# Sums of weight pieces and of hidden tiles, placed elsewhere in six passes of a fused attention and mixture-of-experts kernel

## The chip, the cores and the metric

The kernel runs on one core of one Trainium2 chip. The metric is the time of one execution on the device in microseconds, the median of several runs. A core has TensorE (PE: matmuls into PSUM banks), VectorE (DVE), ScalarE (ACT), GpSimd (POOL) and SyncE (SP), whose queue issues all of this kernel's DMA transfers in order. Each engine works through its own list of instructions in order and waits on semaphores of the others.

## The reference

```python
def _attn_ref(q, k, v):                       # B, H, S, D = 8, 8, 576, 64; chunk = 64
    scores = scale * np.matmul(q_c, k_c.transpose(0, 1, 2, 4, 3))
    scores = scores - np.max(scores, axis=-1, keepdims=True)
    attn = np.exp(scores)
    attn = attn / (np.sum(attn, axis=-1, keepdims=True) + 1e-09)
    out = np.matmul(attn, v_c)
...
def _moe_ref(x, domain_probs, w1, w2):        # N, D, E, F = 4608, 512, 4, 1024
    p = domain_probs / (domain_probs.sum(-1, keepdims=True) + 1e-09)
    out = np.zeros((N, D), dtype=np.float32)
    for e in range(E):
        h = np.maximum(x @ w1[e], 0.0)
        out += p[:, e:e + 1] * (h @ w2[e])
```

Attention within chunks of 64 positions gives 4608 tokens of 512 numbers. Each token goes through all four experts, and the results are added with the token's weights.

## The kernel before, in words

**Tiling.** A block is 512 tokens. The first block is computed plainly; the other eight go in four pairs (0 to 3). An expert's 1024 hidden units are halved, so that there are 8 passes over weight halves for each pair: passes 0 to 7 are the first block's, 8 to 15 pair 0's, 16 to 23 pair 1's, and so on to 39. A matmul in full precision is made of three: every factor is split into a high part (a rounded copy, on ScalarE) and a low part (what is left, a subtraction on GpSimd).

**Seven products for eight.** A pass multiplies 2x2 blocks by a scheme of seven products with sums of blocks on both sides. Each product is six matmuls of 128x512. For w1 the factors are `a11 a12 a22` and the sums `s1 s2 s3 s4`, for two groups g = 0, 1 of columns (the first and second half). A w1 *unit* holds two such factors with their high and low parts. There are seven units (0 to 6) to a pass: unit 0 is a11 and a12 of the first half, unit 1 is s2 and s1, unit 2 is s3 and a22, unit 3 is s4 and a11 of the second half, and so on. For the hidden tiles h, the sums are `t1` to `t4`, each for k = 0, 1.

**The order of a pass.** TensorE's 28 steps are written out: `a1 g1 a2 g2 g6 a5 g5 a6 a3 g7 a7 g4 g3 a4 h1 h2 b1 b5 h6 b6 b3 h5 b7 h7 b2 b4 h4 h3`, numbered 0 to 27. g and h are the first layer (x by w1) of this pass, in banks A0, B0, C0; a and b are the second layer (h by w2) of the pass before, in banks A1, B1, C1. In a and b, products 1, 6, 7 and 4 accumulate in A1, one after the other, product 2 goes to B1, and 5 and 3 to C1; after each step VectorE adds the bank to a sum in SBUF (`acc`, L936). TensorE may write a bank again only when that addition has read it. So b4 (step 25) waits for b7's addition (step 22), and a1 of the next pass for b4's.

**What stands beside the steps.** A table `at` says after which step other work is written: each engine's list follows this order exactly. In h's part, L909 adds two banks, L874 applies the rectifier and the token's weight, L880 is a sum t1 to t4, and L886 and L889 are high and low parts of h. Attention for the next pair runs beside passes 10 to 14 (scores on TensorE, softmax on VectorE and ScalarE: L275, L280, L286, L289 to L296, L155, L161, L165).

**What is special in passes 9 to 15.** In these the kernel makes w1's units on the chip from raw w1 pieces and stores them in memory, so that later passes only load them. `half_load` brings a half's pieces, `half_sum` (L525, 128x256) makes s1 to s4 from them, `make_unit` takes a unit's high part on ScalarE (L542) and low part on GpSimd (L543), and a store follows (L546). Units 0 and 1 of the next pass are made at steps 20 and 26, unit 2 of this pass at step 2, and the others at 8, 11, 14 and 17. g6 (step 4) is the first reader of unit 1. The pieces of the first half are summed one pass ahead, those of the second half in their own pass. All pieces lie in the tile `xraw`, in which q and k for attention (L189) and w2's raw pieces take the same room afterwards. In pass 14, `make_before` splits three units of the last w2 (ScalarE L558, GpSimd L559, stores L563). In pass 15 the tokens of pair 1 come back from memory into `xraw` (L270), and VectorE makes a first sum of them at step 5 (L657).

Of the kernel before, what the change touches and what calls it, by code (L numbers as in the profile page):

```python
# [31 lines left out]
def chunk_attention_moe(ctx: ExitStack, tc: tile.TileContext, qk, v, v0, dp, w1, w2, out):  # L32
# [10 lines left out]
    nc = tc.nc  # L43
# [3 lines left out]
    n_pass = 2 * n_exp  # L47
# [96 lines left out]
    def a_softmax(t):  # L144
        a_less_max(t)
        a_exps(t)
# [10 lines left out]
    def a_place(t, name="pt"):  # L157

        s = st[t]
        s["pt"] = att.tile([P, 2, HG, C], F32, name=name)  # L160
        nc.scalar.copy(out=s["pt"], in_=s["sc"])  # L161
        for half in range(2):
            for i in range(2):
                here, there = (slice(half * C + k * B, half * C + (k + 1) * B) for k in (i, 1 - i))
                nc.scalar.copy(  # L165
                    out=s["pt"][there, :, :, i * B : (i + 1) * B],
                    in_=s["sc"][here, :, :, (1 - i) * B : (2 - i) * B],
                )
# [11 lines left out]
    def two_load(t, i, groups=slice(0, 2)):  # L180
        if i == 0:
            a_load(t)
            return
        pair = (t - NT) // (PAIR * NT)
        if pair == 1:
            if groups.start == 0:
                to = pieces(0, 4).rearrange("p a b c -> p (a b c)")
                st[t] = {"x": to.rearrange("p (g x h s) -> p g x h s", g=2, x=2, h=HG)}
            nc.sync.dma_start(  # L189
                out=st[t]["x"][:, groups],  # L190
                in_=qk[t, groups].rearrange("g c d x h s -> (c d) g x h s"),
            )
            return
        to = of_tiles(pair, 6, 2).rearrange("p g (x i) (j s) -> p g x (i j) s", x=2, s=C)
        st[t] = {"x": to}
        nc.sync.dma_start(out=to, in_=qk[t].rearrange("g c d x h s -> (c d) g x h s"))

    def two_load_v(t, i, odd):
        if i and not odd:
            pair, j = divmod(t - NT, PAIR * NT)  # L200
            if pair == 1:
                to = pieces(4, 2).rearrange("p a b c -> p (a b) c")
            else:
                to = of_tiles(pair, 7 if j == 7 else 5, 1)[:, 0]
            st[t]["v"] = to.rearrange("p j (h d) -> p j h d", h=2)
        elif not odd:
            st[t]["v"] = load.tile([P, NK, 2, C], F32, name="v_in")
        to = st[t]["v"].rearrange("p (g i) h d -> p g i h d", i=2)
        of = v[t - NT].rearrange("p (g i h) d -> p g i h d", g=2, i=2)
        if not odd:  # L210
            nc.sync.dma_start(out=to[:, :, 0], in_=of[:, :, 0])
            return
        for half in range(2):
            rows, other = slice(half * C, (half + 1) * C), slice((1 - half) * C, (2 - half) * C)
            nc.sync.dma_start(out=to[rows, :, 1], in_=of[other, :, 1])
# [12 lines left out]
    def two_weights(t):  # L228
        two_sums(t, "B1")
        a_scale(t)  # L230
        a_transpose(t)
# [282 lines left out]
    def half_load(n, g, fs=(0, 1)):  # L514
        if not scratch:
            scratch.append(xpool.tile([P, NK * PAIR * SUB], F32, name="xraw"))
        for f in fs:
            cols = slice((2 * f + g) * P, (2 * f + g + 1) * P)
            to = pieces(7 * g + AT[f"a{f + 1}1"], 2)
            nc.sync.dma_start(out=to.rearrange("p a b c -> p (a b) c"), in_=of_pass(w1, n)[:, :, cols])  # L520

    def half_sum(g, name, eng=None):
        a, b, op = SUMS[name]
        to, a, b = (pieces(7 * g + AT[i], 1)[:, 0] for i in (name, a, b))
        (eng or nc.vector).tensor_tensor(out=to, in0=a, in1=b, op=op)  # L525
# [45 lines left out]
    def make_next(i):  # L571
        keep_made()
        if making[i]:
            making[i].pop(0)()
# [337 lines left out]
    class Outer:  # L912
# [17 lines left out]
        def add(self, src, i, s):  # L930
            key = self.n // n_pass, 2 * i + self.g + NK * s
            if key not in acc:
                acc[key] = opool.tile([P, SUB], F32, name=f"acc{key[1]}")
                nc.scalar.copy(out=acc[key], in_=src)
            else:
                nc.vector.tensor_tensor(out=acc[key], in0=src, in1=acc[key], op=ALU.add)  # L936
# [101 lines left out]
    def outputs(pair, m, s):  # L1038

        stage = []  # L1040

        def begin():
            stage.append(att.tile([P, SUB], F32, name=("e", "pt")[s]))
            nc.vector.transpose(stage[0], acc[pair + 1, m + NK * s])
            put_out(pair, m, s, stage[0], (0, 1))

        return begin, lambda: put_out(pair, m, s, stage[0], (2, 3))
# [12 lines left out]
    sc, es, pt, av = {}, {}, {}, {}  # L1060
# [62 lines left out]
    first = slice(0, GT * P)  # L1123
# [417 lines left out]
    def first_load(pair):  # L1541
        if pair < n_pairs:
            a_load((1 + pair * PAIR) * NT)
# [3 lines left out]
    def attend_two(at, pair, r):  # L1547

        t0 = (1 + pair * PAIR) * NT
        if pair == 1:  # L1550
            if 0 <= r <= 3:
                for g, i in enumerate((22, 27)):
                    add(at, i, lambda g=g: two_load(t0 + 2 * r + 1, 1, slice(g, g + 1)))
            if 1 < r <= 5:
                for odd in range(2):
                    add(at, 3 + odd, lambda odd=odd: two_load_v(t0 + 2 * r - 3, 1, odd))
        elif r == 0:
            add(at, 12, lambda: two_load(t0 + 1, 1))
        if not 1 <= r <= 5:
            return  # L1560
        t, burst = t0 + 2 * (r - 1), 13 if pair == 1 else 12
        if r > 1:
            add(at, 6, lambda: two_weights(t - 1))
            add(at, 9, lambda: a_place(t - 1, "e"))
        add(at, burst, lambda: two_next(t - 2 if r > 1 else None, t if r < 5 else None))
        if r < 5:
            add(at, burst + 1, lambda: a_softmax(t))
            add(at, 17, lambda: two_weights(t))
            add(at, 21, lambda: a_place(t), lambda: a_softmax(t + 1))
            for i in range(1 if pair == 1 else 2):  # L1570
                for odd in range(2):
                    add(at, burst + 2 + 2 * i + odd, lambda i=i, odd=odd: two_load_v(t + i, i, odd))
                if r < 4:
                    add(at, burst + 6 + i, lambda i=i: two_load(t + 2 + i, i))
# [46 lines left out]
    def half_sums(at, g, places, eng=None):  # L1621
        for i, name in zip(places, SUMS):
            if i is not None:
                add(at, i, lambda name=name: half_sum(g, name, eng))
# [3 lines left out]
    def later_pass(n, ahead, late, held):  # L1628

        first_pass, last_pass = n % n_pass == 0, n % n_pass == n_pass - 1  # L1630
        pair, more = n // n_pass - 1, n + 1 < n_run
        at, first = {}, {}
        left, sc = Units(n), Scaled(n)
# [22 lines left out]
        put(24, "b22", 1)  # L1656
        put(26, "b21", 1)
        crowded = n == 2 * n_pass - 1
        if more and not crowded:
            add(at, 26, lambda: sc.sum("t4", 0, nc.gpsimd))  # L1660
        add(at, 27, lambda: sc.sum("t1", 1), lambda: sc.sum("t3", 1))
        for i, f in later:
# [6 lines left out]
            attend_two(at, pair + 1, n % n_pass)  # L1669
        elif pair == 0:  # L1670
            attend_two(at, pair + 1, n % n_pass - 1)
        late = []
        if n + 1 < 2 * n_pass - 1:
            add(at, 5 if n == n_pass + 1 else 13, lambda: half_load(n + 1, 0))
            add(at, 13, lambda: half_load(n + 1, 1, (0,)))
            add(at, 19, lambda: half_load(n + 1, 1, (1,)))
            half_sums(at, 0, (15 if n == n_pass + 1 else 20, 21, 21, 21))
        if n_pass < n < 2 * n_pass - 1:
            if n == n_pass + 1:
                half_sums(first, 1, (5, 6, 9, 10))  # L1680
                half_sums(first, 0, (None, None, None, 3))
            else:
                half_sums(first, 1, (9, 9, 10, 11), nc.gpsimd)
            for i in (3, 8, *MAKE_AT[2:]) if n == n_pass + 1 else MAKE_AT:
                add(at, i, lambda: make_next(0))
        if n == 2 * n_pass - 2:
            for k, i in enumerate((11, 15, 18)):
                add(at, i, lambda k=k: make_before(k))
        for m, makes, raws in (
            (2 * n_pass - 2, (), ((3, None, 0), (4, None, 2), (10, None, 6))),  # L1690
# [11 lines left out]
        if first_pass and pair > 0:  # L1702
            for i in range(4):
# [3 lines left out]
            late = [  # L1707
                (1 + apart * i + after, f) for i in range(4)
                for after, f in enumerate(outputs(pair - 1, 1 + 2 * (i // 2), i % 2))
            ]  # L1710
        if last_pass and more:
            xs = []

            def x(what, *args):
                return lambda: getattr(xs[0], what)(*args)
# [10 lines left out]
            if not crowded:  # L1726
# [3 lines left out]
            late = [  # L1730
                (0, x("hi", "b22")), (9 if crowded else 0, lambda: first_load(pair + 2)), (5 if crowded else 1, x("lo", "t3")),
                (7 if crowded else 6, x("lo", "t4")), (8, x("lo", "b22")),
            ]
# [143 lines left out]
```

## Time and profile before

| What | Value |
|---|---|
| median of 3 runs | 1470.11 us (1470.1 to 1470.32) |
| profiled execution | 1472.01 us |
| its span, first to last instruction | 1470.2 us |
| TensorE busy in the span | 1455.7 us (99%) |
| VectorE, ScalarE, GpSimd busy | 1069.0, 624.5, 986.2 us |
| granted TensorE clock | 1.0 |

Rows of the timeline begin with the start in us from the span's start, then the duration in us, the engine, the line in the kernel before, the operation, the tile written and the tiles read (without buffer numbers), the shapes and the count. In brackets stands the idle time before it and what ended it. Consecutive equal instructions share a row. A row of the waits gives engine, line and tile, what was waited for, the sum in us, the count and the longest. A row of the stretches gives the stretch, its length, the busy us and instructions of TensorE, its weight loads, VectorE, ScalarE and GpSimd, then the granted clock, the share of the DMA engines and GB/s.

### The profile page before, as it was taken

What the parts mean: (1) busy time and instruction counts of PE and PEld (TensorE: products, weight loads), DVE (VectorE), ACT (ScalarE), POOL (GpSimd) and SP (SyncE); (2) the same over time, 40 slices, a digit from 0 to 9 for tenths busy, and PEclk for the clock granted to TensorE, in tenths of its full rate; (3) what the DMA queues carried; (4) which work ended last, traced back from release to release, by engine and by line L of the source; (5) the groups of instructions that cost most, each with busy time, mean ns of one, the idle gap of its engine ahead of it and who ended that gap; (6) DMA issues with size and microseconds to landing.
All of it is one profiled execution on the core that took longest, in us unless ns stands there. A gap on an engine that the chain in (4) does not pass through costs nothing.

```text
span 1470.2 us, 23417 instructions
## 1 busy us (share of the span) xinstructions
PE 1455.7 (99%) x8574; PEld 1197.1 (81%) x8574; DVE 1069.0 (73%) x1480; ACT 624.5 (42%) x1169; POOL 986.2 (67%) x748
## 2 busy tenths in 40 slices
PE   9999999999999999999999999999999999999998
PEld 7888887877778788888888888888888888888887
DVE  6566768788887886777767977777668866666665
ACT  5556535444544434444423435444334343233332
POOL 6878889888779684555557656555557655555555
PEclk9999999999999999999999999999999999999999
DMA  9899697768779779766565788675556695665655
GB/s 324 306 340 324 244 351 238 235 214 265 255 239 319 258 237 266 247 201 233 191 212 189 230 228 271 228 241 190 206 196 203 198 255 200 196 208 192 208 189 157
DMA packets 198995, 348.52 MB, mean 237 GB/s; under 512 B 70224, under 2 KB 109408, under 8 KB 198496
## 3 DMA queue, kind: packets, MB, share of 16 engines
q1 hardware_dynamic: 198880, 347.02, 72.3%
q8 instruction: 68, 1.11, 0.3%
q14 instruction: 47, 0.39, 0.1%
HBM read 275.59 MB, written 71.38 MB: 236 GB/s over the span
## 4 chain that ended last, share of the span: by engine, by line
PE 88%; POOL 4%; DVE 3%; DMA 2%; ACT 1%; issue 1%; SPq 0%; POOLq 0%; ACTq 0%; DVEq 0%
PE A L711 45%; PE C L711 25%; PE B L711 14%; POOL hf L889 1%; PE psa L222 1%; POOL hf L400 1%; POOL wf L543 1%; PE B L241 1%; DMA w<-xraw 1%; DMA xraw<-x_kept 1%; DVE wraw L880 1%; ACT pt L165 0%; DMA wf<-w 0%; DVE acc L936 0%; ACT hf L886 0%
## 5 line engine op out<-in xcount | busy, mean ns | idle before, releaser
L889 POOL TENSOR_TENSOR hf<-wraw,hf 128x512 fp32r<-128x512 f32 x384 | 507.5, 1341 | 232.3 <-ACT hf L886 231.0
L711 PE MATMUL A<-hf,wf 128*128 128x512 f32 x1536 | 392.2, 391 | 6.0 <-DVE acc L936 6.0
L711 PE MATMUL A<-xh,wf 128*128 128x512 f32 (+1 forms) x1120 | 388.1, 390 | 1.8 <-POOL wf L543 1.8
L886 ACT CAST hf<-wraw 128x512 fp32r<-128x512 f32 x384 | 233.4, 622 | 301.8 <-DVE wraw L880 108.0
L711 PEld LDWEIGHTS A<-hf,wf 128*128 128x128 f32 x1536 | 285.9, 188 | 69.8 <-DVE acc L936 10.3
L711 PEld LDWEIGHTS A<-xh,wf 128*128 128x128 f32 x1120 | 209.6, 188 | 47.8 <-POOL wf L543 4.2
L774 ACT COPY s<-A 128x512 f32<-128x512 f32 x192 | 112.6, 587 | 287.8 <-PE A L711 287.1
L711 PE MATMUL A<-xl,wf 128*128 128x512 f32 (+1 forms) x560 | 217.5, 388 | 0.0
L936 DVE TENSOR_TENSOR acc<-A,acc 128x512 f32<-128x512 f32 x232 | 157.7, 680 | 66.0 <-PE A L711 65.7
L711 PE MATMUL C<-xh,wf 128*128 128x512 f32 (+1 forms) x584 | 201.1, 388 | 0.1
L711 PE MATMUL C<-hf,wf 128*128 128x512 f32 x768 | 194.8, 389 | 0.0
L711 PEld LDWEIGHTS C<-hf,wf 128*128 128x128 f32 x768 | 144.2, 188 | 30.0
L711 PEld LDWEIGHTS C<-xh,wf 128*128 128x128 f32 x584 | 109.5, 188 | 22.9 <-DVE B L909 0.5
L889 POOL TENSOR_TENSOR hf<-wf,hf 128x512 fp32r<-128x512 f32 x64 | 89.2, 1393 | 54.6 <-ACT hf L886 54.6
L880 POOL TENSOR_TENSOR wf<-wraw,wf 128x512 f32<-128x512 f32 x31 | 40.0, 1289 | 127.7 <-DVE wf L874 126.9
L711 PEld LDWEIGHTS A<-xl,wf 128*128 128x128 f32 x560 | 105.2, 188 | 21.7
L711 PE MATMUL B<-xh,wf 128*128 128x512 f32 (+1 forms) x344 | 115.5, 384 | 0.0
L936 DVE TENSOR_TENSOR acc<-C,acc 128x512 f32<-128x512 f32 x120 | 82.6, 689 | 42.9 <-PE C L711 40.1
L711 PE MATMUL C<-xl,wf 128*128 128x512 f32 (+1 forms) x292 | 113.2, 388 | 0.0
L880 DVE TENSOR_TENSOR wraw<-wf,wraw 128x512 f32<-128x512 f32 x64 | 95.1, 1486 | 7.1 <-POOL hf L889 6.0
L711 PE MATMUL B<-hf,wf 128*128 128x512 f32 x384 | 97.7, 389 | 0.0
L880 POOL TENSOR_TENSOR wraw<-wraw 128x512 f32<-128x512 f32 x63 | 93.1, 1478 | 0.0
(247 smaller groups left out, 1989.0 us busy)
## 6 DMA issues: line engine op xcount, KB each, us to landing
wf<-w SPq DMA_DIRECT2D x402, 512.0 KB, 4.2
w<-wf SPq DMA_DIRECT2D x46, 512.0 KB, 5.3
w<-hf SPq DMA_DIRECT2D x28, 512.0 KB, 6.6
w<-hf SPq DMA_DIRECT2D x42, 256.0 KB, 4.9
wf<-in_w SPq DMA_DIRECT2D x19, 512.0 KB, 5.8
qk_in<-in_qk SPq DMA_DIRECT2D x16, 512.0 KB, 6.9
xraw<-in_qk SPq DMA_DIRECT2D x14, 512.0 KB, 7.5
ws<-p_t SPq DMA_DIRECT2D x24, 256.0 KB, 4.1
```

The source lines that it names most:

```text
L222: nc.tensor.matmul(s["sc"][of_half(half), c, slot], lhsT=q, rhs=k, start=True, stop=True)
L241: nc.tensor.matmul(av[half][of_half(slot % 2), i, head // 2], lhsT=s["v"][of_half(half), head // 2, head % 2], rhs=s["pt"][of_half(half), ...
L400: eng.tensor_tensor(out=t[1], in0=src, in1=t[0].bitcast(F32), op=ALU.subtract)
L543: nc.gpsimd.tensor_tensor(out=t[:, :, 1], in0=src, in1=t[:, :, 0].bitcast(F32), op=ALU.subtract)
L711: nc.tensor.matmul(out, lhsT=lhs(k, a), rhs=rhs(k, b), start=first and i == 0, stop=last and i == len(parts) - 1, skip_group_check=not (fi ...
L774: nc.scalar.copy(out=t, in_=self.a)
L880: (eng or nc.vector).tensor_tensor(out=self.values[place, k], in0=self.values[a, k], in1=self.values[b, k], op=op)
L886: nc.scalar.copy(out=self.part(name, 0)[:, k], in_=self.values[name, k])
L889: (eng or nc.gpsimd).tensor_tensor(out=self.part(name, 1)[:, k], in0=self.values[name, k], in1=self.part(name, 0)[:, k].bitcast(F32), op=A ...
L936: nc.vector.tensor_tensor(out=acc[key], in0=src, in1=acc[key], op=ALU.add)
```

## The change

Four places change, all in passes 9 to 14.

1. In passes 10 to 13 the sums s2, s3 and s4 of the next pass's first half go from step 21 to steps 23, 23 and 24 (s1 stays at step 20). The half load of q and k that overwrites those pieces goes from step 22 to 25.
2. In passes 9 to 13 the sum t4 of h (k = 0) goes from step 26 to step 0 of the next pass, which puts it behind unit 1's low part on GpSimd.
3. In pass 14 the three units of the last w2 are made at steps 10, 13 and 16 instead of 11, 15 and 18.
4. In passes 10 to 14 the four sums of the second half's pieces (steps 9, 9, 10 and 11) go from GpSimd to VectorE.

```diff
         if pair == 1:
             if 0 <= r <= 3:
-                for g, i in enumerate((22, 27)):
+                for g, i in enumerate((25, 27)):
                     add(at, i, lambda g=g: two_load(t0 + 2 * r + 1, 1, slice(g, g + 1)))
...
         crowded = n == 2 * n_pass - 1
-        if more and not crowded:
+        w1_made = n_pass < n < 2 * n_pass - 2
+        if more and not crowded and not w1_made:
             add(at, 26, lambda: sc.sum("t4", 0, nc.gpsimd))
...
-        late = []
+        late = [(0, lambda: sc.sum("t4", 0, nc.gpsimd))] if w1_made else []
         if n + 1 < 2 * n_pass - 1:
...
-            half_sums(at, 0, (15 if n == n_pass + 1 else 20, 21, 21, 21))
+            half_sums(at, 0, (15, 21, 21, 21) if n == n_pass + 1 else (20, 23, 23, 24))
         if n_pass < n < 2 * n_pass - 1:
+            half_sums(first, 1, (5, 6, 9, 10) if n == n_pass + 1 else (9, 9, 10, 11))
             if n == n_pass + 1:
-                half_sums(first, 1, (5, 6, 9, 10))
                 half_sums(first, 0, (None, None, None, 3))
-            else:
-                half_sums(first, 1, (9, 9, 10, 11), nc.gpsimd)
...
         if n == 2 * n_pass - 2:
-            for k, i in enumerate((11, 15, 18)):
+            for k, i in enumerate((10, 13, 16)):
                 add(at, i, lambda k=k: make_before(k))
```

How this moves instructions is seen at three places. The first is VectorE at the end of pass 10, from the softmax's subtraction (L280) to h4's rectifier (L874 from bank A). `acc_2931` is b7's addition, `acc_2917` b2's, and `acc_3036` (in the changed kernel `acc_3035`) b4's. Before:

```order
L280 TENSOR_TENSOR psa<-psa,m_3369 128x2x256
L525 TENSOR_TENSOR xraw<-xraw 128x256 x3
L936 TENSOR_TENSOR acc_2931<-A_3280,acc_2931 128x512
L880 TENSOR_TENSOR wraw<-wraw 128x512
L909 TENSOR_TENSOR B_3396<-C_3356,s_3397 128x512
L874 SCALAR_TENSOR_TENSOR wraw<-B_3396,ws 128x512
L936 TENSOR_TENSOR acc_2917<-B_3405,acc_2917 128x512
L936 TENSOR_TENSOR acc_3036<-A_3280,acc_3036 128x512
L874 SCALAR_TENSOR_TENSOR wraw<-A_3251,s_2946 128x512
```

In the changed kernel:

```order
L280 TENSOR_TENSOR psa<-psa,m_3369 128x2x256
L936 TENSOR_TENSOR acc_2931<-A_3280,acc_2931 128x512
L880 TENSOR_TENSOR wraw<-wraw 128x512
L909 TENSOR_TENSOR B_3392<-C_3356,s_3393 128x512
L874 SCALAR_TENSOR_TENSOR wraw<-B_3392,ws 128x512
L525 TENSOR_TENSOR xraw<-xraw 128x256 x2
L936 TENSOR_TENSOR acc_2917<-B_3403,acc_2917 128x512
L525 TENSOR_TENSOR xraw<-xraw 128x256
L936 TENSOR_TENSOR acc_3035<-A_3280,acc_3035 128x512
L874 SCALAR_TENSOR_TENSOR wraw<-A_3251,s_2946 128x512
```

The three sums stood ahead of b7's addition; now two stand ahead of b2's and one ahead of b4's.

The second is GpSimd at the end of pass 9 and the start of pass 10 (each boundary up to pass 14's start looks alike): low parts of h (L889), t4 (L880) and unit 1's low part (L543, `wf_3050`, in the changed kernel `wf_3049`). Before:

```order
L889 TENSOR_TENSOR hf_2969<-wraw,hf_2969 128x512
L889 TENSOR_TENSOR hf_3023<-wraw,hf_3023 128x512
L880 TENSOR_TENSOR wraw<-wraw 128x512
L543 TENSOR_TENSOR wf_3050<-xraw,wf_3050 128x2x256
L889 TENSOR_TENSOR hf_3012<-wraw,hf_3012 128x512
```

In the changed kernel:

```order
L889 TENSOR_TENSOR hf_2969<-wraw,hf_2969 128x512
L889 TENSOR_TENSOR hf_3022<-wraw,hf_3022 128x512
L543 TENSOR_TENSOR wf_3049<-xraw,wf_3049 128x2x256
L880 TENSOR_TENSOR wraw<-wraw 128x512
L889 TENSOR_TENSOR hf_3011<-wraw,hf_3011 128x512
```

The unit's low part and the sum have changed places; what follows is the same.

The third is SP's queue late in pass 14: stores of w1's units 5 and 6 (`w_0_5`, `w_0_6`) and of w2's units 1 and 2 (`w_1_1`, `w_1_2`, two transfers each), and loads for pass 15 (L601). Before:

```order
L546 DMA w_0_5_186<-wf_5014 128x1024
L563 DMA w_1_1_203<-qk_in 256x1x256
L563 DMA w_1_1_203<-xraw 256x1x256
L601 DMA wf_5064<-w_0_0_195 128x1024
L601 DMA wf_5078<-w_1_0_188 128x1024
L546 DMA w_0_6_187<-wf_5055 128x1024
L563 DMA w_1_2_204<-v_in 256x1x256
L563 DMA w_1_2_204<-xraw 256x1x256
```

In the changed kernel:

```order
L601 DMA wf_5038<-w_1_6_180 128x1024
L546 DMA w_0_5_186<-wf_5018 128x1024
L563 DMA w_1_2_204<-v_in 256x1x256
L563 DMA w_1_2_204<-xraw 256x1x256
L601 DMA wf_5069<-w_0_0_195 128x1024
L601 DMA wf_5080<-w_1_0_188 128x1024
L546 DMA w_0_6_187<-wf_5060 128x1024
```

w2's last unit is stored ahead of w1's last unit and of two loads; after these rows four loads and then the tokens' return (L270) stand in both.

## The prediction

> **What bounds the kernel now.** TensorE. I read the page first, then stretches that hold one pass each, then TensorE's waits in passes 9 to 15, then the engines' rows around each wait.
>
> ```profile
> span 1470.2 us, 23417 instructions
> PE 1455.7 (99%) x8574; PEld 1197.1 (81%) x8574; DVE 1069.0 (73%) x1480; ACT 624.5 (42%) x1169; POOL 986.2 (67%) x748
> ```
> ```profile
> 309.64:352.37 42.73, 41.08 (x298) 33.24 (x297) 34.45 (x53) 21.54 (x44) 34.57 (x29) 1.00 0.79 259
> 600.18:640.59 40.41, 40.41 (x298) 33.47 (x297) 31.38 (x47) 17.59 (x36) 22.07 (x17) 1.00 0.66 223
> ```
> ```profile
> PE A L711 <- DVE acc L936: 6.0, 5, 1.3
> PE A L711 <- POOL wf L543: 1.8, 4, 0.5
> ```
>
> The two stretches run from one step a5 to the next of pass 11, and over a pass of the second pair. Both hold 298 TensorE instructions at full granted clock; the first is 42.73 - 40.41 = 2.3 us longer. Passes 9 to 14 make w1's units on the chip; that extra work makes TensorE wait. The waits between 225 and 530 us are few: five behind a VectorE addition (four in passes 10 to 13, one in pass 15), four behind the low part of a w1 unit. Each term below follows one of these to where it goes. A step of six matmuls takes 1.36 us.
>
> **The b4 wait, and the three sums moved behind it.** End of pass 10; VectorE, GpSimd, ScalarE, TensorE in this order:
>
> ```profile
> 290.27 0.67 DVE L880 TENSOR_TENSOR wraw<-wf,wraw 128x512 f32<-128x512 f32 x1
> ...
> 295.45 0.70 DVE L280 TENSOR_TENSOR psa<-psa,m 128x512 f32<-128x512 f32 x1
> 296.06 1.08 DVE L525 TENSOR_TENSOR xraw<-xraw 128x256 f32<-128x256 f32 x3
> 297.06 0.68 DVE L936 TENSOR_TENSOR acc<-A,acc 128x512 f32<-128x512 f32 x1
> 297.66 1.71 DVE L880 TENSOR_TENSOR wraw<-wraw 128x512 f32<-128x512 f32 x1
> 299.30 0.69 DVE L909 TENSOR_TENSOR B<-C,s 128x512 f32<-128x512 f32 x1
> 300.02 0.69 DVE L874 SCALAR_TENSOR_TENSOR wraw<-B,ws 128x512 f32<-128x512 f32 x1
> 300.63 0.68 DVE L936 TENSOR_TENSOR acc<-B,acc 128x512 f32<-128x512 f32 x1
> 301.22 0.68 DVE L936 TENSOR_TENSOR acc<-A,acc 128x512 f32<-128x512 f32 x1
> ```
> ```profile
> 294.40 1.29 POOL L543 TENSOR_TENSOR wf<-xraw,wf 128x512 fp32r<-128x512 f32 x1
> ...
> 297.55 1.28 POOL L889 TENSOR_TENSOR hf<-wf,hf 128x512 fp32r<-128x512 f32 x1 [1.84 <-ACT hf L886]
> 300.11 5.05 POOL L889 TENSOR_TENSOR hf<-wraw,hf 128x512 fp32r<-128x512 f32 x4 [1.28 <-ACT hf L886]
> ```
> ```profile
> 297.37 0.58 ACT L774 COPY s<-A 128x512 f32<-128x512 f32 x1
> ```
> ```profile
> 295.08 1.52 PE L711 MATMUL B<-hf,wf 128*128 128x512 f32 x6
> 297.80 1.67 PE L711 MATMUL A<-hf,wf 128*128 128x512 f32 x6 [1.19 <-DVE acc L936]
> 302.05 1.57 PE L711 MATMUL A<-hf,wf 128*128 128x512 f32 x6
> ```
>
> b2 starts at 295.08 and b4, due at 296.44, only at 297.80, when b7's addition (297.06) has left bank A1. Three sums of pieces stand before that addition: 1.00 us (296.06 to 297.06). Without them the addition ends at 296.74, b4 starts about 296.80, and TensorE is 1.00 us ahead.
>
> But the sums move into a place that is no emptier. Two of them now stand ahead of b2's addition (300.63) and the third ahead of b4's (301.22), which frees A1 for a1, the next pass's first step. In the trace a1 starts at 302.05, right as that addition ends (301.90). It has no slack, and becomes what is late next.
>
> What a sum costs there depends on GpSimd. At 296.06 GpSimd stood idle (295.69 to 297.55). Elsewhere the same instruction looks like this, VectorE's rows first (the fastest, median and slowest in ns; three in pass 9), then GpSimd's beside them:
>
> ```profile
> L525 DVE TENSOR_TENSOR xraw<-xraw x25: 412/419/1510, 231.5 to 424.9; 128x256 f32<-128x256 f32 x25
> 252.18 3.71 DVE L525 TENSOR_TENSOR xraw<-xraw 128x256 f32<-128x256 f32 x3
> 251.46 2.72 POOL L889 TENSOR_TENSOR hf<-wraw,hf 128x512 fp32r<-128x512 f32 x2
> ```
>
> With GpSimd busy, three sums took 3.71 us instead of 1.08, and the slowest one 1.51. L880 shows the same: 0.67 us with GpSimd idle (290.27), 1.71 beside a GpSimd operation (297.66). That one ended at 299.37, which is 0.54 after the GpSimd operation's end at 298.83. So a VectorE operation that reads two SBUF tiles waits for the running GpSimd operation to end, then runs; additions that read PSUM stay at 0.68.
>
> I lay out VectorE anew from 296.06. b7's addition ends 296.74; the L880 meets an idle GpSimd, 296.66 to 297.33. L909 waits for ScalarE's copy (297.95) and ends 298.67, L874 299.40. GpSimd takes its operation of 297.55 to 298.83 and then, since its next input is ready earlier, goes on without the gap of 1.28 us: low parts end near 300.08, 301.5 and 303.0. The first sum arrives at 299.32 and ends at 300.36 (300.08 + 0.28); the second takes 1.51, to 301.80; b2's addition goes to 302.41; the third sum arrives at 302.33 amid the next low part and ends 303.24; b4's addition ends 303.85. So a1 starts at 303.91 instead of 302.05: 1.86 us later than before, the gained 1.00 included. A restart after such a wait costs another 0.13 (b4 to the next step: 1.49 instead of 1.36, here too).
>
> Bounds: with all three sums at the idle price (0.34) b4's addition ends at 301.65 and a1 starts 0.34 earlier than before; with all three at 1.51 it ends at 304.9 and a1 starts 2.9 later. I take 1.86: GpSimd has four low parts in a row there, and must.
>
> [...]
>
> **The g6 wait, and the sum of h behind the low part.** TensorE's g6 in pass 11, and GpSimd before it:
>
> ```profile
> 307.56 0.39 PE L711 MATMUL A<-xh,wf 128*128 128x512 f32 x1
> ...
> 308.61 0.73 PE L711 MATMUL A<-xh,wf 128*128 128x512 f32 x2 [0.43 <-POOL wf L543]
> ...
> 309.64 0.62 PE L711 MATMUL C<-hf,wf 128*128 128x512 f32 x2
> ```
> ```profile
> 305.10 1.76 POOL L880 TENSOR_TENSOR wraw<-wraw 128x512 f32<-128x512 f32 x1
> 306.82 1.74 POOL L543 TENSOR_TENSOR wf<-xraw,wf 128x512 fp32r<-128x512 f32 x1
> ```
>
> g6 takes 309.64 - 307.56 = 2.08 instead of 1.36: 0.72 lost, because the low part ends at 308.56 behind the sum (t4, 305.10). With the sum behind it, and a1 at 303.91, the last low part of h ends about 306.4, VectorE's L880 takes its turn to 306.97, and the unit's low part ends 308.2; g6 then begins at 309.4. No wait is left. t4's sum ends about 310.0, before the tile it reads is overwritten (L874, about 311.8). So 0.72 gained at each of four boundaries, and 0.2 in pass 10, whose g6 waits less.
>
> **Second half's sums on VectorE.** Step 9 on in pass 11, VectorE, GpSimd, TensorE's a4:
>
> ```profile
> 318.12 0.69 DVE L874 SCALAR_TENSOR_TENSOR wraw<-B,ws 128x512 f32<-128x512 f32 x1
> ```
> ```profile
> 317.74 1.29 POOL L543 TENSOR_TENSOR wf<-xraw,wf 128x512 fp32r<-128x512 f32 x1
> 318.99 2.93 POOL L525 TENSOR_TENSOR xraw<-xraw 128x256 f32<-128x256 f32 x4
> ```
> ```profile
> 320.52 1.30 PE L711 MATMUL A<-hf,wf 128*128 128x512 f32 x5
> ```
>
> Here GpSimd ends its low part at 319.03 and the next needs the second of these very sums, so the first ends near 319.3, the second 319.7, and a7's addition 320.35, just before a4 needs bank A1 at 320.52. The other two may take 1 us each; their next reader on TensorE is h1, at 324.06. Cost 0, bounds 0 and 1.9 a pass (both at 1.51). [...]
>
> The half load of q and k that moves from step 22 to 25 waits on SP's queue for the third sum (303.3 instead of 297.2). The w1 store and loads behind it follow at once; the next load in that queue went out at 309.0 anyway. Cost 0.
>
> **w2's units sooner.** Pass 15 loses 1.4 us at a7: bank A1 waits for an addition queued behind a sum that needs x back from memory. TensorE, then the DMA rows:
>
> ```profile
> 485.49 1.65 PE L711 MATMUL A<-hf,wf 128*128 128x512 f32 x6 [1.25 <-DVE acc L936]
> ```
> ```profile
> 455.00:473.00 18.00, 18.00 (x81) 14.88 (x81) 13.10 (x18) 7.61 (x13) 16.71 (x14) 1.00 1.01 362
> SPq L601 <- DMA w<-wf: 3.3, 2, 2.3
> SPq L270 <- DMA w<-xraw: 0.9, 1, 0.9
> ```
> ```profile
> 459.18 1.75 POOL L543 TENSOR_TENSOR wf<-xraw,wf 128x512 fp32r<-128x512 f32 x1
> 460.90 1.29 POOL L559 TENSOR_TENSOR xraw<-xraw,v_in 128x512 fp32r<-128x512 f32 x1
> ```
>
> The third w2 unit (L559) and the last w1 unit (L543) change places: one is stored 1.3 us sooner, the other as much later. x's return waits for both, directly (0.9) and through the load ahead of it in SP's queue (2.3 of the 3.3). The DMA engines are full (1.01) from 455 to 473, so order alone brings little. I take -0.3, bounds -1.5 and +1.0.
>
> **Sum.** Four boundaries: 1.86 + 0.13 - 0.72 = +1.27 each, +5.1. Pass 10's g6 -0.2, pass 15 -0.3. Together +4.6 on a span of 1470.2. The profiled execution took 1472.0, 1.8 around its span; the runs' median is 1470.11. So 1476.6 for an execution like the profiled one, and 1474.7 for the median.
>
> **Rivals.** *The sums run as fast as they do now* (faster): 0.34 each, a1 at 301.7, so -0.34 + 0.13 - 0.72 = -0.9 a boundary, -3.7, with -0.2 and up to -1.4 in pass 15: 1465. For it: the median of 25 such sums is 419 ns. Against: those ran beside an idle GpSimd. *The loss is only moved* (no change): the sums hit the ends of GpSimd's operations and wait 1 us in all instead of 2.3; a1 at 302.6, +0.55 + 0.13 - 0.72 = 0: 1470. *The second half's sums hit GpSimd as well* (slower still): a7's addition ends at 322.4 and a4 waits 1.9 in five passes, +9.5 on top: 1484; against it, GpSimd has nothing to run there.
>
> **How the numbers follow.** Forecast 0.55, moved 0.20, clean sums 0.18, both halves hit 0.07. About 0.2% (2.9 us) is what a measurement of this kernel can tell from no change: faster 0.18, same 0.20, slower 0.62. The forecast's own range is 1472.5 to 1478; the 8-in-10 range reaches into the clean case and one contended half pass more, 1465 to 1480.
>
> **What would show it.** b4's wait shrinks from 1.2 to about 0.3 us; a new wait of 2 to 3 us stands at a1 behind VectorE's addition in passes 11 to 14; L525 on VectorE has a mean near 1 us before it; the wait on L543 is gone; pass 15's a7 still waits. If a1 follows h3 without a gap, my layout is wrong.

## The result, and the profile after

The changed kernel takes 1480.88 us in the median of 6 runs (1479.09 to 1483.08); the kernel before, in 6 runs, 1470.35 (1470.1 to 1471.88). The ratio is 1.0069, with a 95% interval of 1.0056 to 1.0082: slower by 10.5 us. The forecast was 1474.7, with a range from 1465.0 to 1480.0; the measured median lies 0.9 us outside it. The profiled execution went from 1472.01 to 1479.82 us.

First the head of the page of the changed kernel, then TensorE's waits between 225 and 530 us (line, tile, what was waited for, sum, count, longest):

```profile
span 1478.0 us, 23431 instructions
PE 1458.6 (99%) x8574; PEld 1198.9 (81%) x8574; DVE 1081.3 (73%) x1500; ACT 623.5 (42%) x1169; POOL 973.1 (66%) x728
```
```profile
PE A L711 <- DVE acc L936: 12.7, 9, 2.7
```

The wait on L543 is gone. The waits behind VectorE's additions grew from 6.0 us in five to 12.7 in nine, with a longest of 2.7. But TensorE's busy time also rose, from 1455.7 to 1458.6 us, with the same 8574 matmuls. That can't come from waiting. Stretches that hold passes 11, 12 and 13, each from its a1 to the next (stretch, length, busy time of TensorE, weight loads, VectorE, ScalarE, GpSimd, then the granted clock, DMA share and GB/s), first before, then after:

```profile
302.05:344.73 42.68, 41.07 (x297) 33.21 (x297) 34.40 (x52) 21.53 (x43) 34.52 (x29) 1.00 0.75 248
344.73:387.46 42.73, 41.08 (x297) 33.24 (x297) 34.45 (x52) 21.60 (x43) 34.61 (x29) 1.00 0.79 256
387.46:430.23 42.77, 41.10 (x297) 33.24 (x297) 34.46 (x52) 21.53 (x43) 34.59 (x29) 1.00 0.71 235
```
```profile
303.66:349.13 45.47, 42.63 (x296) 34.45 (x296) 36.90 (x56) 21.31 (x43) 32.23 (x24) 0.96 0.73 237
349.13:394.53 45.40, 42.52 (x296) 34.40 (x297) 36.89 (x56) 21.32 (x43) 32.22 (x24) 0.96 0.73 238
394.53:438.56 44.03, 41.16 (x296) 33.18 (x296) 37.08 (x56) 21.32 (x43) 32.27 (x24) 1.00 0.75 245
```

The granted clock of the changed kernel is 0.96 in passes 11 and 12 and 1.00 in pass 13; in the kernel before it is 1.00 in all three. The two passes with the lower clock are 1.4 us longer than the third. Here is the whole account by passes, each from a1's start to the next a1's, worked out from TensorE's timeline; the forecast's column has the prediction's own terms, each in the pass in which it falls:

| Pass | before | after | difference | forecast |
|---|---|---|---|---|
| 10 | 41.21 | 43.02 | +1.81 | 1.86 - 0.2 = +1.66 |
| 11 | 42.68 | 45.47 | +2.79 | 1.86 + 0.13 - 0.72 = +1.27 |
| 12 | 42.73 | 45.40 | +2.67 | +1.27 |
| 13 | 42.77 | 44.03 | +1.26 | +1.27 |
| 14 | 40.24 | 39.68 | -0.56 | 0.13 - 0.72 = -0.59 |
| 15 | 39.77 | 39.77 | 0.00 | -0.3 |
| sum | 249.40 | 257.37 | +7.97 | +4.58 |

(Pass 10 starts 0.2 us sooner after, so the span grows by 7.8.) Passes 10, 13 and 14 come out within 0.15 us of the forecast. The miss lies in passes 11 and 12, 2.9 us together, and in pass 15, 0.3.

**What the clock did.** TensorE around the boundary from pass 10 to pass 11 in the changed kernel:

```profile
296.60 1.66 PE L711 MATMUL A<-hf,wf 128*128 128x512 f32 x6 [0.19 <-DVE acc L936]
...
303.66 2.19 PE L711 MATMUL A<-hf,wf 128*128 128x512 f32 x6 [2.69 <-DVE acc L936]
305.65 0.63 PE L711 MATMUL A<-xh,wf 128*128 128x512 f32 x1
```

b4 now waits 0.19 instead of 1.19, and a1 waits 2.69: the wait that was foretold. But a1's six matmuls take 2.19 us instead of 1.57, and a single matmul after them 0.63 instead of 0.39. The trace holds two stretches at half clock (below called falls), from 304.56 and from 348.93 us, each recorded at 3.413 us. They start 44.37 us apart, 13.0 times that length, so I cut the time into steps of 3.413 us that end where the falls begin (below the grid); that such steps run on between the falls is an estimate of mine from that distance. In the changed kernel, the step ahead of each fall and the step of the fall; then, for the boundaries into passes 13 and 14, the step in which TensorE was least busy and the one behind it:

```profile
301.14:304.56 3.42, 0.90 (x4) 0.77 (x5) 3.42 (x6) 0.32 (x1) 1.58 (x2) 1.00 0.23 36
304.56:307.97 3.41, 3.41 (x10) 2.64 (x9) 3.31 (x4) 0.82 (x2) 3.03 (x3) 0.50 0.52 202
...
345.52:348.93 3.41, 0.95 (x5) 0.45 (x3) 3.41 (x5) 0.00 (x0) 2.67 (x2) 1.00 0.54 217
348.93:352.34 3.41, 3.21 (x8) 2.53 (x9) 3.31 (x6) 1.14 (x2) 1.94 (x2) 0.50 0.68 237
...
389.89:393.30 3.41, 1.95 (x9) 1.29 (x7) 3.41 (x5) 0.62 (x1) 3.41 (x3) 1.00 0.80 311
393.30:396.72 3.42, 2.19 (x10) 1.80 (x11) 3.35 (x6) 1.14 (x2) 1.21 (x2) 1.00 0.49 152
...
434.26:437.68 3.42, 1.61 (x8) 1.00 (x6) 3.42 (x4) 0.51 (x1) 3.37 (x3) 1.00 0.87 296
437.68:441.09 3.41, 2.53 (x11) 2.09 (x12) 3.34 (x6) 1.14 (x2) 1.25 (x1) 1.00 0.06 22
```

All four boundaries hold the same wait of about 2.7 us. Where it lay inside one step, TensorE was busy for 0.90 or 0.95 us of 3.41, and the next step ran at half clock. Where it was spread over two steps, TensorE was busy for 1.61 us or more in each, and the clock stayed. By a pass length each fall cost about 1.4 us (45.47 and 45.40 against 44.03; in the two other traces with falls, below, 1.2 to 1.7).

### The profile page after: what moved, and what is told of

It is laid out like the page before. It is cut to its first block, busy times and chain, and to the rows that moved or that the text cites. A ratio compares the mean times of both kernels' runs of the same rounds, so it can differ in the third digit from the quotient of the medians.

```text
span 1478.0 us, 23431 instructions
## 1 busy us (share of the span) xinstructions
PE 1458.6 (99%) x8574; PEld 1198.9 (81%) x8574; DVE 1081.3 (73%) x1500; ACT 623.5 (42%) x1169; POOL 973.1 (66%) x728
## 4 chain that ended last, share of the span: by engine, by line
PE 91%; DVE 3%; DMA 2%; ACT 1%; issue 1%; POOL 1%; SPq 0%; ACTq 0%; POOLq 0%
PE A L711 48%; PE C L711 25%; PE B L711 15%; PE psa L222 1%; DVE xraw L525 1%; PE B L241 1%; POOL wf L400 1%; DMA wf<-in_w 1%; DVE acc L936 1%; DMA wf<-w 0%; POOL hf L400 0%; ACT pt L165 0%; ACT hf L886 0%; DMA v_in<-in_v 0%; DMA xraw<-in_qk 0%
## 5 line engine op out<-in xcount | busy, mean ns | idle before, releaser
L889 POOL TENSOR_TENSOR hf<-wraw,hf 128x512 fp32r<-128x512 f32 x384 | 507.9, 1341 | 237.4 <-ACT hf L886 236.0
L711 PE MATMUL A<-hf,wf 128*128 128x512 f32 x1536 | 394.7, 393 | 12.7 <-DVE acc L936 12.7
L936 DVE TENSOR_TENSOR acc<-A,acc 128x512 f32<-128x512 f32 x232 | 157.7, 680 | 66.6 <-PE A L711 66.1
L880 POOL TENSOR_TENSOR wf<-wraw,wf 128x512 f32<-128x512 f32 x31 | 40.0, 1289 | 136.5 <-DVE wf L874 135.7
L889 POOL TENSOR_TENSOR hf<-wf,hf 128x512 fp32r<-128x512 f32 x64 | 89.7, 1402 | 54.9 <-ACT hf L886 54.9
L936 DVE TENSOR_TENSOR acc<-C,acc 128x512 f32<-128x512 f32 x120 | 82.6, 689 | 46.0 <-PE C L711 43.1
L880 DVE TENSOR_TENSOR wraw<-wf,wraw 128x512 f32<-128x512 f32 x64 | 94.0, 1469 | 7.2 <-POOL hf L889 6.1
L880 POOL TENSOR_TENSOR wraw<-wraw 128x512 f32<-128x512 f32 x63 | 92.8, 1472 | 0.0
```

Source lines behind the costliest of these rows:

```text
L711: nc.tensor.matmul(out, lhsT=lhs(k, a), rhs=rhs(k, b), start=first and i == 0, stop=last and i == len(parts) - 1, skip_group_check=not (fi ...
L880: (eng or nc.vector).tensor_tensor(out=self.values[place, k], in0=self.values[a, k], in1=self.values[b, k], op=op)
L889: (eng or nc.gpsimd).tensor_tensor(out=self.part(name, 1)[:, k], in0=self.values[name, k], in1=self.part(name, 0)[:, k].bitcast(F32), op=A ...
```

## The experiments

All compare with runs of the kernel before on the same chip: 1471.49 us (19 runs) for the first four, 1471.08 (16 runs) for the others. Pass lengths are read as in the table above, and what a step loses is its time over 1.36 us, from its start to the next one's.

**The sums back, the rest of the change kept.** Is it the moved sums alone that cost?

```diff
-                for g, i in enumerate((25, 27)):
+                for g, i in enumerate((22, 27)):
...
-            half_sums(at, 0, (15, 21, 21, 21) if n == n_pass + 1 else (20, 23, 23, 24))
+            half_sums(at, 0, (15 if n == n_pass + 1 else 20, 21, 21, 21))
```

> The changed kernel with its first edit undone: s2, s3, s4 of the first half back at step 21, the half load back at 22; the other three edits stay. My theory (the sums behind b7's addition cause all of the loss, the waits at a1 and, through them, the lower clock): b4 waits 1.2 us again in passes 10 to 13, no wait at a1, no wait at g6, clock 1.0 throughout: 4 x 0.74 + 0.2 = 3.2 us under the kernel before, about 1467. Rival (the second half's sums on VectorE, or t4 behind the low part, cause a good part of the loss): 1474 or more.

Measured: 1471.55 us, ratio 1.0002 (0.9993 to 1.0012). The loss is gone, and so is the gain that I expected from the sum behind the low part. TensorE's waits in this kernel, and its step a5 in pass 11:

```profile
PE A L711 <- DVE acc L936: 4.8, 4, 1.2
PE C L711 <- POOL hf L889: 1.4, 4, 0.4
```
```profile
308.69 1.07 PE L711 MATMUL C<-hf,wf 128*128 128x512 f32 x4
310.11 0.72 PE L711 MATMUL C<-hf,wf 128*128 128x512 f32 x2 [0.36 <-POOL hf L889]
```

b4's four waits are back. g6 no longer waits for L543, but a5, the step behind it, now waits for the low part of h that t4's sum delays: 0.63 to 0.65 us a pass where g6 had lost 0.72 to 0.76. Pass lengths 41.16, 42.74, 42.75, 42.77, 40.28 are the kernel before's within 0.1. So edits 2, 3 and 4 together change nothing in passes 10 to 14: edit 2 moves a wait by one step and makes it 0.1 us smaller, and a4 loses 0.10 to 0.14 us more in each pass, which is edit 4's price (shown further down). In the changed kernel a5's wait is hidden only because TensorE itself arrives late.

**The moved sums alone, in the kernel before.** This is edit 1 without the others, the half load included.

> The kernel before with the first edit alone. My theory: the a1 wait of 2.7 us in front of passes 11 to 14, as in the changed kernel, with part of the g6 wait kept (about 0.3 each): 4 x (1.27 + 0.3) = +6, and the clock at half for 3.4 us after two to four of these waits, 1.7 us each: 1479 to 1483. Rival (the loss needs the other edits): 1470 to 1473.

Measured: 1479.03 us, ratio 1.0058 (1.0041 to 1.0075), as expected. Edit 1 by itself carries the loss. a1 waits as in the changed kernel (the eight waits on L936 make 11.5 us, the longest 2.7). But of g6's wait, of which 0.3 us a pass should have stayed, hardly anything is left, although t4 still stands ahead of the unit's low part. GpSimd and g6 at the start of pass 13, whose a1 starts at 393.15:

```profile
395.68 1.75 POOL L880 TENSOR_TENSOR wraw<-wraw 128x512 f32<-128x512 f32 x1
397.39 1.74 POOL L543 TENSOR_TENSOR wf<-xraw,wf 128x512 fp32r<-128x512 f32 x1
```
```profile
399.18 0.73 PE L711 MATMUL A<-xh,wf 128*128 128x512 f32 x2
```

g6 loses 0.13 to 0.15 us in passes 12 to 14, where it lost 0.74 to 0.76 in the kernel before. The late a1 alone takes away some 0.6 of it. Passes 13 and 14 are 44.02 and 39.71 us, against 44.03 and 39.68 in the changed kernel, which has edits 2 to 4 as well.

This trace has one fall. Its steps, cut in the same way: the one ahead of the fall, the fall, and the least busy one at the boundary into pass 14:

```profile
299.92:303.33 3.41, 1.18 (x6) 0.64 (x4) 3.41 (x5) 0.09 (x1) 2.94 (x3) 1.00 0.33 125
303.33:306.74 3.41, 2.94 (x7) 2.36 (x8) 3.34 (x5) 1.14 (x2) 1.67 (x2) 0.50 0.72 226
...
433.04:436.45 3.41, 1.48 (x7) 0.90 (x5) 3.41 (x5) 0.34 (x1) 3.19 (x3) 1.00 0.90 305
```

A fall came behind the step with 1.18 us of busy time, none behind the step with 1.48.

**TensorE kept busy in the wait.** Is the clock the missing term? The changed kernel, with ten extra matmuls into the free bank B0 behind step 27 of passes 10 to 13; nothing reads their result.

```diff
             getattr(steps[name[0]], f"p{name[1]}")()
+            if i == 27 and n_pass + 1 < n < 2 * n_pass - 2:
+                spare = bank("B0")
+                for _ in range(10):
+                    nc.tensor.matmul(spare, lhsT=xt[0][0][:, 0, :P], rhs=xt[0][0][:, 0], start=True, stop=True)
```

> The changed kernel with ten extra matmuls of 128x512 into the free bank B0 behind step 27 of passes 10 to 13, while a1 waits (2.3 of its 2.7 us); their result is not used. Theory (TensorE's idle time in front of a1 brings the clock down, and that is what my forecast left out): granted clock 1.0 in the whole span, spread of the runs gone, time 1470.35 + 4.4 = about 1475, the waits at a1 else the same. Rival (the clock falls for another reason, or the extra loss is elsewhere): 1479 to 1483 as the changed kernel, with clock under 1.

Measured: 1477.26 us, ratio 1.004 (1.0025 to 1.0055); expected were about 1475 and no spread, and the four runs go from 1476.16 to 1478.7. TensorE of this kernel at the same boundary, and its passes 11 to 13:

```profile
300.74 2.43 PE L1740 MATMUL B<-xh 128*128 128x512 f32 x10
303.64 1.66 PE L711 MATMUL A<-hf,wf 128*128 128x512 f32 x6 [0.47 <-DVE acc L936]
```
```profile
303.64:347.70 44.06, 43.42 (x306) 35.04 (x306) 37.14 (x56) 21.30 (x43) 32.31 (x24) 1.00 0.75 245
347.70:391.82 44.12, 43.48 (x307) 35.05 (x307) 37.18 (x56) 21.33 (x43) 32.34 (x24) 1.00 0.74 245
391.82:435.87 44.05, 43.40 (x306) 35.04 (x306) 37.12 (x56) 21.31 (x43) 32.30 (x24) 1.00 0.75 245
```

a1 starts at 303.64, as late as without the extra work (303.66), since VectorE sets it. But the clock is 1.00, a1 takes 1.66 us, and passes 11 and 12 have the length of pass 13. That is not luck with the grid: in passes 10 to 14 the least busy 3.41 us of TensorE, wherever a step is laid, still hold 2.94 us of work, against 0.72 in the changed kernel. With more work the kernel comes out at 1477.26 against 1479.57 for the changed kernel on this chip (below). The two intervals overlap, so it is the pass lengths that show it: 44.06 and 44.12 against 45.47 and 45.40. What is left over the kernel before, 5.8 us with an interval from 3.7 to 8.1, is the wait itself: passes 10 to 14 of the two traces, 215.0 and 209.6 us, differ by 5.4.

**The three sums on GpSimd, at step 21.** If VectorE's turn behind GpSimd is what costs, the sums could go where they were before, but on the other engine.

```diff
-            half_sums(at, 0, (15, 21, 21, 21) if n == n_pass + 1 else (20, 23, 23, 24))
+            half_sums(at, 0, (15, 21, 21, 21) if n == n_pass + 1 else (20, None, None, None))
+            if n > n_pass + 1:
+                half_sums(at, 0, (None, 21, 21, 21), nc.gpsimd)
```

> The changed kernel with s2, s3, s4 of the first half back at step 21, but on GpSimd, which stands idle there for 1.85 us; s1 stays on VectorE at step 20, the half load at 25. Theory (they fit into GpSimd's gap, 3 x 0.72 = 2.2 us, and VectorE is 1 us shorter ahead of b7's addition): b4's wait falls from 1.49 to 0.5, none at a1 and g6: 4 x 1.0 + 3.2 = 7.2 us under the kernel before, about 1463. Rival (GpSimd is then late with h's low parts, or VectorE's t1 sum waits for it and moves b4's addition out): a wait at a1 of 0.5 to 1 us, 1465 to 1467.

Measured: 1469.48 us, ratio 0.9986 (0.9977 to 0.9996). It is quicker than the kernel before, by 2.0 us, but not by the 7.2 that a clean move would give. GpSimd at the end of pass 10 in this kernel, and TensorE's waits:

```profile
295.81 2.56 POOL L525 TENSOR_TENSOR xraw<-xraw 128x256 f32<-128x256 f32 x3
298.33 1.30 POOL L889 TENSOR_TENSOR hf<-wf,hf 128x512 fp32r<-128x512 f32 x1
299.58 5.52 POOL L889 TENSOR_TENSOR hf<-wraw,hf 128x512 fp32r<-128x512 f32 x4
```
```profile
PE A L711 <- DVE acc L936: 2.0, 5, 1.3
PE C L711 <- POOL hf L889: 1.1, 4, 0.3
PE B L711 <- POOL hf L889: 0.8, 4, 0.2
```

GpSimd's gap there was 1.86 us in the kernel before (295.69 to 297.55). Three sums take 2.56, the first low part of h starts 0.8 us later, and four more stand behind it without a gap. b4's wait falls to 0.36 us a pass, but a2 and a5 of the next pass now wait for low parts, 0.47 and 0.55 us at each boundary. So the first half of the rival came true, that GpSimd is late with the low parts; but the wait stands at a2 and a5 and not at a1, and the time lies outside both ranges.

**The changed kernel again**, for the clock and for pass 15.

> The changed kernel once more, beside the others on one chip. Theory (four waits of 2.7 us at a1, of which some bring the clock to half for 3.4 us): 7 to 12 us over the kernel before, spread over 2 to 4 us by whole falls of the clock of 1.7 us each. Rival (the extra loss was that first chip's): 4 to 5 us, without spread.

Measured: 1479.57 us, ratio 1.0059 (1.0045 to 1.0073), with granted clocks from 0.995 to 0.998 in four runs, 1478.6 to 1482.21 us: as expected. Passes 10 to 14 take 217.95 us in its trace, 8.3 more than in the kernel before, which is the whole difference here. The falls stand at the same two boundaries (from 304.44 and 348.81), after steps in which TensorE was busy for 1.04 and 0.81 us. Nothing in the traces ties the grid to the kernel, so that looks like chance: they start 0.9 and 1.0 us after pass 11's a1 in the two executions of the changed kernel, and 0.5 us before it with the sums moved alone. A third stretch at half clock begins at 1475.21 us, where the work ends, 343.0 steps behind the first. Pass 15 has no wait at a7 this time; TensorE's a7 in the first trace, and here:

```profile
493.26 1.66 PE L711 MATMUL A<-hf,wf 128*128 128x512 f32 x6 [1.25 <-DVE acc L936]
```
```profile
492.10 1.67 PE L711 MATMUL A<-hf,wf 128*128 128x512 f32 x6
```

One kernel has that wait in one execution and not in another. The traces of before, of after and of the sums on GpSimd have it, the others not, among them the kernel with the sums moved alone, which leaves w2's units where they were.

**The sum of h one step later still.** With the sums of pieces back, t4 at step 1 instead of 0 puts it behind the low part that a5 waits for.

```diff
-        late = [(0, lambda: sc.sum("t4", 0, nc.gpsimd))] if w1_made else []
+        late = [(1, lambda: sc.sum("t4", 0, nc.gpsimd))] if w1_made else []
```

> As e1_sums_back (first edit undone), but t4's sum goes one step further back, to step 1 of the next pass, behind the low part of t1 that a5 reads. In e1_sums_back the wait at g6 was gone but 0.64 us stood at a5 instead. Theory (t4's 1.3 us on GpSimd moves the wait to whichever low part stands behind it): a5's wait goes too, 4 x 0.64 = 2.6 us under the kernel before. Rival (GpSimd as a whole is late there, the wait moves on to g5 or a6): no change.

Measured: 1471.83 us, ratio 1.0004 (0.9995 to 1.0014). This is the rival: the wait goes on to a6 (0.42 to 0.45 us) and g3 (0.2); the pass lengths stay those of the kernel before (41.19, 42.83, 42.84, 42.78, 40.29). As long as b4 waits 1.2 us behind the sums, moving t4 only chooses who waits.

**The sums split between the engines.** s1 and s2 at step 20 on VectorE, s3 and s4 at step 21 on GpSimd, whose gap holds two. It differs from the run with three sums there in a second thing: t4 is at step 1. Edits 3 and 4 are kept.

```diff
-            half_sums(at, 0, (15, 21, 21, 21) if n == n_pass + 1 else (20, 23, 23, 24))
+            half_sums(at, 0, (15, 21, 21, 21) if n == n_pass + 1 else (20, 20, None, None))
+            if n > n_pass + 1:
+                half_sums(at, 0, (None, None, 21, 21), nc.gpsimd)
```

> First half's sums split: s2 with s1 on VectorE at step 20, where VectorE waits 1.4 us for ScalarE; s3 and s4 on GpSimd at step 21, where it is idle 1.85 us; t4 at step 1 of the next pass; edits 3 and 4 kept. Theory (each engine has room for so much and no more at this place: in e4_sums_gpsimd three sums of 0.72 overran GpSimd's gap and the low parts were late at a2 and a5): b4 waits 0.36, a2 and a5 0 to 0.2, a1 0: 4 x (1.0 + 0.6) = 6 us under the kernel before. Rival (VectorE's two sums delay the softmax by 1.4 us, b4 waits longer): no gain.

Measured: 1466.53 us (5 runs, 1466.16 to 1466.63), ratio 0.9967 (0.9954 to 0.9979): 4.6 us quicker than the kernel before, of the 6 expected, and the quickest here together with the next. VectorE and GpSimd at the end of pass 10, and all of TensorE's waits between 225 and 530 us:

```profile
292.12 2.49 DVE L525 TENSOR_TENSOR xraw<-xraw 128x256 f32<-128x256 f32 x2
294.60 0.69 DVE L275 TENSOR_REDUCE m<-psa 128x8 f32<-128x512 f32 x1
...
295.94 0.68 DVE L936 TENSOR_TENSOR acc<-A,acc 128x512 f32<-128x512 f32 x1
```
```profile
295.72 1.43 POOL L525 TENSOR_TENSOR xraw<-xraw 128x256 f32<-128x256 f32 x2
297.43 1.42 POOL L889 TENSOR_TENSOR hf<-wf,hf 128x512 fp32r<-128x512 f32 x1 [0.28 <-ACT hf L886]
```
```profile
PE A L711 <- DVE acc L936: 0.8, 4, 0.2
```

The two sums on GpSimd fit its gap with 0.28 us to spare. The two on VectorE cost 2.49 us beside a busy GpSimd, but at a place ahead of the softmax where no bank waits for them, and the softmax (L275) starts no later than before (294.60 against 294.73), against the rival. b7's addition starts at 295.94 instead of 297.06, and a1 without a wait. Passes 10 to 14 are 40.23, 41.67, 41.70, 41.60 and 40.11 us, together 4.3 less than before. That is b4's wait, 1.0 in each of passes 10 to 13, and little else: the rest of the wait behind t4 and the low parts has gone on to a6 (0.32) and g3 (0.2), which the list of TensorE's waits doesn't show and the expectation left out.

**The same, with the tokens' sum of pass 15 at step 7 instead of 5.**

```diff
-            add(at, 5, lambda: xs.append(Tokens(pair + 1)), x("sum1"))
+            add(at, 7 if crowded else 5, lambda: xs.append(Tokens(pair + 1)), x("sum1"))
```

> e10_split_sums, and pass 15's first sum of returned tokens (L657) after step 7 instead of 5, behind a6's addition, so that a7 does not wait for the tokens' return. Theory: where e10_split_sums loses 1.4 us at a7 this does not; 0 to 1.4 us under e10_split_sums. Rival (the sum then delays a3's addition and the wait moves to a later step): the same time as e10_split_sums.

Measured: 1466.79 us, ratio 0.9969 (0.9957 to 0.998): no difference from the kernel without it. a7 did not wait there either, so the question could not be put.

## Why the prediction was right and wrong

**The layout of VectorE held to 0.25 us.** VectorE at the end of pass 10 in the changed kernel, then GpSimd:

```profile
295.86 0.68 DVE L936 TENSOR_TENSOR acc<-A,acc 128x512 f32<-128x512 f32 x1
296.46 0.68 DVE L880 TENSOR_TENSOR wraw<-wraw 128x512 f32<-128x512 f32 x1
...
299.13 2.47 DVE L525 TENSOR_TENSOR xraw<-xraw 128x256 f32<-128x256 f32 x2
301.53 0.68 DVE L936 TENSOR_TENSOR acc<-B,acc 128x512 f32<-128x512 f32 x1
302.13 0.88 DVE L525 TENSOR_TENSOR xraw<-xraw 128x256 f32<-128x256 f32 x1
302.93 0.68 DVE L936 TENSOR_TENSOR acc<-A,acc 128x512 f32<-128x512 f32 x1
```
```profile
298.61 4.12 POOL L889 TENSOR_TENSOR hf<-wraw,hf 128x512 fp32r<-128x512 f32 x3
```

This trace runs 0.2 us ahead of the one before. Forecast were L880 at 296.66 (here 296.46) for 0.67, the two sums from 299.32 to 301.80 (299.13 to 301.60), the third ending at 303.24 (303.01), b4's addition at 303.85 (303.61) and a1 at 303.91 (303.66). The three sums took 3.35 us where they had taken 1.08. The third of them, from 302.13 to 303.01, ended 0.28 us behind the GpSimd operation that ran until 302.73. So the step "an operation that reads two SBUF tiles waits for the running GpSimd operation to end" held here, and with it the +1.86.

**b4 gains 1.00**: right (1.19 to 0.19). **The restart costs 0.13**: right in size; a1 takes 1.49 us in passes 13 and 14. But it took 1.43 before, so only 0.06 of it is new.

**g6's 0.72 at each boundary**: right in the sum, by luck. The prediction booked it for edit 2, the sum behind the low part. With edit 1 alone the late a1 takes some 0.6 of it away and edit 2 adds the last 0.13 to 0.15; with a1 on time edit 2 gave 0.1, since a5's wait took the place of g6's. The step looked at what t4's reader needs and not at the low part that is queued behind it, nor at how much of the wait a TensorE that arrives later would see.

**The second half's sums cost 0**: nearly. VectorE, then TensorE's a4 and its weight loads, in pass 13 of the changed kernel, which runs at full clock:

```profile
411.64 0.68 DVE L936 TENSOR_TENSOR acc<-A,acc 128x512 f32<-128x512 f32 x1
```
```profile
412.38 1.66 PE L711 MATMUL A<-hf,wf 128*128 128x512 f32 x6
412.38 1.22 PEld L711 LDWEIGHTS A<-hf,wf 128*128 128x128 f32 x6 [0.27 <-DVE acc L936]
```

The addition ends at 412.32, when a4's weight load already waits for it, and a4 loses 0.14 us against the kernel before; forecast was an end 0.17 ahead of a4. In passes 11 and 12 of this trace, behind the falls, a4 loses nothing. The kernel with edit 1 alone loses nothing at a4, and the one with edits 2 to 4 alone 0.10 to 0.14 a pass. So the price is 0.1 us a pass, near the lower bound of 0 to 1.9, and most of the 0.15 by which pass 10 exceeds its forecast. **The half load costs 0**: nothing in passes 10 to 14 speaks against it, and the quickest kernel here keeps it at step 25.

**Pass 15's -0.3**: nothing in the profiled pair (39.77 in both). a7's wait comes and goes from one execution to the next, with and without edit 3, so what edit 3 does to it stays open. It wasn't tried alone.

**What failed is the sum: it has no term for TensorE's clock.** All that it books for what comes after a1's wait is the restart of 0.13. It took every matmul behind the wait at the price of the trace of before, where the clock is 1.00 in all these passes. I forecast a wait of nearly 3 us at four boundaries and did not ask what such a wait does to TensorE. Two of the four brought 3.41 us at half clock, 2.9 us together in the profiled execution. That execution was forecast at 1476.6 and took 1479.82; the clock is 2.9 of the 3.2 us between, pass 15 the other 0.3.

The median is further off, 6.2 us. With the same two terms the forecast would have been 1477.9, inside the range; the other 3.0 us stay open, and more falls are only part of an answer. 0.998 is the granted clock of the profiled execution with its two falls (2 x 3.41 x 0.5 / 1478 = 0.0023). But the second profiled execution has two falls as well and shows 0.997, since the stretch at half clock at its end adds to them. So the four runs at 0.997 may have had two falls or three, and their times go from 1479.09 to 1482.1. Only the run at 0.995 (1483.08 us) must have lost more, some 15 us at half clock, an estimate that makes about four falls. The kernel with the sums back, whose granted clock is 0.999 or 1.0, spreads over 2.9 us too (1470.84 to 1473.77), of which a7's wait could be 1.3. What separates the runs beyond that isn't shown. In the later session the loss was 8.5 us, and two falls explain it.

Of the rivals, the clean sums are ruled out (2.47 us for two) and the moved loss too, and contention in the second half cost 0.1 us a pass and not 1.9. The time lay between the forecast and the last of them, for a reason that none of them named.

## What to carry to other kernels

Price a new wait twice: by its length, and by what it does to the clock of the work behind it (here 2.9 us behind two of four such waits). Where a wait would leave TensorE idle for 2.7 us, as here, look at how busy it is in stretches of 3.4 us (at most 1.18 us of work ahead of a fall here, and at least 2.94 with the wait filled, without a fall), and rather spread the wait or fill it.

Work that has to find another place goes where an engine is measured to be idle, in the portion that fits: in a gap of 1.86 us two sums gained 4.6 us (with the third at another idle place and t4 later) and three gained 2.0, and the same three beside a busy neighbour lost 7.5 by themselves, the clock included. And before a gain is booked for an operation that is moved back in a queue, look who is queued behind its new place, and whether the wait would be there at all once the other edits have moved its reader.

## What the runs showed of the hardware

TensorE's clock was at half for 3.41 us behind steps of the same length in which it was busy for 0.81 to 1.18 us (five falls in three traces), and at 1.00 behind the steps shown above with 1.48, 1.61 us or more. No step shown lies between 1.18 and 1.48 us (35% and 43% of its length). Of the four waits of about 2.7 us in the profiled execution of the changed kernel, two left 0.90 and 0.95 us of work in one step and were followed by a fall, and two left 1.95 and 1.61 us in the least busy step and were not. In the second profiled execution the second and third stretches at half clock start 13.0 and 343.0 steps behind the first; between the three traces the first fall started up to 1.5 us elsewhere against a1 of pass 11.

In the changed kernel two sums on VectorE, from 299.13 to 301.60, took 2.47 us while GpSimd ran low parts of 1.4 us each (three in 4.12); in the kernel before, with GpSimd idle, three took 1.08. Two sums on GpSimd in its gap took 1.43.
